# Packed attention with a gated convolution: x of two head groups in one step on eight TensorE tiles, weight parts added on GpSimd

## The chip, the cores and the metric

The kernel runs on one core of a Trainium2 chip. The metric is device time in microseconds for one execution; lower is better. The engines are called as the profile calls them: PE (TensorE's matmuls), PEld (its weight loads), DVE (VectorE), ACT (ScalarE), POOL (GpSimd) and SP (SyncE, which here only issues DMAs). SBUF is the on-chip memory, PSUM the accumulators that PE writes.

## What is computed

```python
# q, k, v: (8, 8, 576, 64)   p: (8, 8, 32, 64)   w_val, w_out: (512, 512)   conv_w: (5, 512)
def sm_attn(qq, kk, vv):
    s = scale * np.matmul(qq, kk.transpose(0, 1, 3, 2))
    a = np.exp(s - np.max(s, axis=-1, keepdims=True))
    a = a / (np.sum(a, axis=-1, keepdims=True) + 1e-09)
    return np.matmul(a, vv)
p_packed = sm_attn(p, k, v)
out = sm_attn(q, p_packed, p_packed)
x = out.transpose(0, 2, 1, 3).reshape(8, 576, 512)
gate = sigmoid(sum(conv_w[k] * xp[:, k:k + 576, :] for k in range(5)))   # xp: x with 4 zero rows in front
return gate * (x @ w_val) @ w_out
```

For each of the 8 batches and 8 heads, 32 packed queries attend to 576 keys (the first attention), the 576 queries attend to the 32 results (the second), and the joined heads x pass through a gated causal convolution between two matrix products. q, k, v and p are 32-bit floats; the three weights reach the kernel as 64-bit floats.

## The kernel before

Heads go in two groups of four (`G` = 2), since four heads of 32 packed rows fill 128 partitions. A batch passes through streams of steps, each named by a letter (and the batch's number) in a table `ORDER`: K, V, Q, P load; `k` and `q` transpose keys and queries on PE (tiles `kpt`, `qpt`) and copy them with ACT; `a` is the first attention (scores `s`, their maxima `nb` on DVE, the exponential on ACT, transposes `at`, products `pv`, the result `ppd`); `p` turns `ppd` into `ppT`; `s` and `t` are the second attention (scores `s` on PE, a transpose of 32x32 blocks to `t` and the maxima `mx` on DVE, a subtraction on POOL, the exponential on ACT, sums `sm` and reciprocals `rs` on DVE, a product on POOL, a transpose back to `a` on DVE and its split into a high part `a2h` and a low part `a2l`); `w` multiplies the packed results by `w_val` (tile `wp`, split into `wph` and `wpl`); `x` computes x itself (function `mixed`, tile `xp`); `g` is the gate (four DVE steps of multiply and add into `sig` after one on ACT, then a tanh, for each of four chunks of 128 channels); `v` is the value product (tile `val`, times `sig`, split into `gvh` and `gvl`); `o` is the output product and its store. L, W, C and O load the weights and convert the 64-bit words: three or four DVE steps per 128 rows make two parts, `top` and `words`, which PE adds into PSUM by two products with the identity (`summed`; tiles `wv_sum` and `wo_sum`).

The order of every engine's instructions is the order of this table: `InOrder` ties each instruction to the one before it on its engine, and a letter in `ORDER` runs one step of its stream (`x0.2` runs two). The engines then run freely, each in its own order, and wait for each other by semaphores. Before the bar `|` in the table the weights' staging memory is alive, behind it `gvh` and `gvl`. SP's DMAs stand in the same order, in one queue.

x is the product of `ppd` (32 packed rows by 64 channels of one head, the weights) and the attention `a` (32 by 288 columns, half the sequence at a time). One head needs a tile of 32 rows and 64 columns of the PE array, of which there are eight: four row groups by two column groups. Before, a step takes the four heads of one group, with head `hl` on row group `hl` and column group `hl % 2`. It writes one buffer of the PSUM ring `big`, which has two buffers of two banks each, and which `scores`, `wp` and `val` use too; ACT then copies it into `xp`. A batch has four such steps and four copies. The ring of `xp` has two tiles, one for each group.

A matmul of 32-bit floats appears as two records in the profile: a step of four x tiles has 8, a step of eight score tiles 16. In the rows that list the instructions in order it is one instruction.

Of the kernel before, what the change touches and what calls it, by code (L numbers as in the profile page):

```python
# [39 lines left out]
 'xp': 2}  # L40
# [6 lines left out]
x0 K0.2 P0 L0.2 Q0 L0.2 V0.2 k0 Q0 L0 k0.2 P1 k0.4 P2 W0 k0.2 W0 K1 k0.2 a0 W0 k0.2 W0 a0 k0 K1 W0.2 a0 W0 L0 a0  # L47
W0 q0 W0 a0 q0.2 W0 q0.2 Q1 a0.3 W0 q0 W0.2 a0 W0 L0 a0 W0 a0.2 W0 a0 W0.5 L0 a0 W0.2 a0.3 V1 W0 a0.6 W0.3 a0 V1
C0 L0 W0 C0 q0 C0 p0 k1 q0 p0 C0 P3 q0 k1 C0 s0 q0 C0 q0 w0 s0 q0 Q1 s0 k1 C0 s0 w0 C0 k1.2 w0 s0.2 k1.2 t0 K2
k1.4 a1 k1 s0 t0 k1 O0 a1 k1 k2 K2 O0 a1.2 P4 t0 O0 t0 x0 a1 k2 q1 O0 a1.3 O0.2 a1 s0 q1 x0 t0 s0 O0 q1 a1 O0.2  # L50
x0 a1 O0 q1 a1 s0 q1 O0 a1 t0 Q2 q1 x0.2 a1 g0 O0 t0 O0.2 a1 V2 a1 t0 O0 g0 a1 t0 x0 O0.2 g0 a1.6 O0 x0 g0 x0 a1
V2 t0 p1 v0 g0 p1 x0 O0 g0 s1 O0 g0 v0 q1 s1 w1 q1 g0 k2 O0.2 w1 s1 g0 s1 k2 w1 O0 k2 q1 O0.2 s1 g0 k2.2 q1.2 O0
K3 k2.2 g0 q1 Q2 a2 k2 O0 x1 g0 s1 t1 k2 g0 q2 k2.2 O0 q2 t1 q2 a2 K3 k2 k3 q2 s1 q2 P5 a2 O0.2 q2 g0 Q3 t1 | v0
g0 a2 t1 x1 s1 O0 k3 v0 s1 k3 x1 a2 k3.2 O0 a2.3 g0 s1 v0 a2 t1 k3 t1 q2 a2 x1 q2 v0 t1 a2 q2 g0 a2 v0 k3 x1 K4
k3 t1 g0 v0.2 q2 g0 v0 q2 a2 Q3 q2 g0 a2 v0 g0 t1 k3 V3 a2.3 k3 t1 k3 a2.2 g0 k3.2 a2.2 k3 v0 K4 v0 a2 g0.2 x1
k4 x1 g1 P6 v0 a2 g1 v0 x1.2 V3 g1 a2 p2 v0 x1 v1 p2 g1.2 o0 g1.2 v1 g1 v1 a3 v1 o0 s2 g1 o0.2 a3 s2 a3 g1 s2 a3
o0 g1 s2 v1 o0 k4 a3 g1 a3.2 x2 q3 v1 s2 a3 s2 a3 t2 q3 k4 v1 w2 k4 s2 t2 g1 k4 v1 q3 w2 v1 s2 k4 q3 w2 s2 k4 q3
k4 K5 o0 t2 q3 Q4 s2 g1 t2 g1 t2 k4 o0 q3 g1 a3 k4 o0.2 q3 t2 a3 g1 t2 g1 k4 g1 v1 a3 x2 o0 t2 a3 o0 a3 v1 g1
# [48 lines left out]
def packed_attention_gated_conv(  # L107
# [97 lines left out]

    def words_of(nm, src, rows):
        words = tile_of("words", [P, DM, 2], U32, f"{nm}_words", stage)[:rows]
        each = rows // len(src)  # L210
        for n, s in enumerate(src):
            sp.dma_start(
                words[n * each : n * each + each].rearrange("a b c -> a (b c)"), s.bitcast(U32)
            )
# [431 lines left out]
```

## Time and profile before

| | |
|---|---|
| median of 3 runs | 319.11 us (318.81 to 319.12) |
| the profiled execution: its time, its span | 318.79 us, 316.7 us |
| PE busy | 292.0 us, 92% |
| PEld busy | 210.3 us, 66% |
| DVE busy | 256.5 us, 81% |
| ACT busy | 211.1 us, 67% |
| POOL busy | 44.8 us, 14% |
| DMA | 43.50 MB, mean 137 GB/s |

The span runs from the first to the last instruction of the profiled execution; its device time holds 2.1 us more. A share of busy time is a mean over stages in which different engines are full. Nearly all instructions are recorded under line 90, the helper that ties them in order, so the rows are told apart by their tiles: `x<-a,ppd` is the product that makes x, `xp<-x` its copy.

### The profile page before, as it was taken

What the parts mean: (1) busy time and instruction counts of PE and PEld (TensorE: products, weight loads), DVE (VectorE), ACT (ScalarE), POOL (GpSimd) and SP (SyncE); (2) the same over time, 40 slices, a digit from 0 to 9 for tenths busy, and PEclk for the clock granted to TensorE, in tenths of its full rate; (3) what the DMA queues carried; (4) which work ended last, traced back from release to release, by engine and by line L of the source; (5) the groups of instructions that cost most, each with busy time, mean ns of one, the idle gap of its engine ahead of it and who ended that gap; (6) DMA issues with size and microseconds to landing.
All of it is one profiled execution on the core that took longest, in us unless ns stands there. A gap on an engine that the chain in (4) does not pass through costs nothing.

```text
span 316.7 us, 7391 instructions
## 1 busy us (share of the span) xinstructions
PE 292.0 (92%) x3028; PEld 210.3 (66%) x3028; DVE 256.5 (81%) x404; ACT 211.1 (67%) x428; POOL 44.8 (14%) x55
## 2 busy tenths in 40 slices
PE   0878987988899999999999999999999999999992
PEld 0534534556766876787777867777787687767871
DVE  0336799999888987898999888997999878868761
ACT  1564787688966778768867786688766955455431
POOL 1000131113002210033003202210032100220000
PEclk9999999999999999999999999999999999999998
DMA  8999999999991479328652866415242021111005
GB/s 180 220 231 226 243 256 218 214 229 192 192 198 74 107 188 224 83 81 216 151 139 73 208 185 120 123 55 129 58 141 68 2 66 36 66 68 47 20 2 167
DMA packets 42476, 43.50 MB, mean 137 GB/s; under 512 B 6085, under 2 KB 36805, under 8 KB 42442
## 3 DMA queue, kind: packets, MB, share of 16 engines
q1 hardware_dynamic: 42442, 43.02, 58.8%
q8 instruction: 24, 0.39, 0.6%
q14 instruction: 10, 0.08, 0.1%
HBM read 33.57 MB, written 9.44 MB: 136 GB/s over the span
## 4 chain that ended last, share of the span: by engine, by line
PE 69%; DVE 15%; ACT 6%; DMA 5%; issue 1%; SPq 0%; POOL 0%; POOLq 0%; DVEq 0%; ACTq 0%
PE o L90 26%; PE val L90 13%; DVE sig L90 6%; PE s L90 5%; PE x L90 5%; PE kpt L90 4%; PE qpt L90 4%; PE pv L90 3%; DMA qm<-in_q_dram 3%; PE at L90 3%; PE wv_sum L90 2%; PE wp L90 2%; DMA p<-in_p_dram 2%; DVE sm L90 2%; ACT sig L90 2%; DVE wo_words L90 1%
## 5 line engine op out<-in xcount | busy, mean ns | idle before, releaser
L90 DVE SCALAR_TENSOR_TENSOR sig<-xp,cw,sig 128x576 f32<-128x576 f32 x128 | 107.5, 840 | 5.9 <-ACT sig L90 4.8
L90 PE MATMUL o<-woh,gvh 128*128 128x512 f32 x144 | 59.0, 409 | 0.1
L90 PE MATMUL o<-wol,gvh 128*128 128x512 f32 x144 | 56.5, 393 | 0.0
L90 PE MATMUL o<-woh,gvl 128*128 128x512 f32 x144 | 56.5, 392 | 0.1
L90 PE MATMUL val<-a2h,wph 128*128 128x288 f32 x128 | 39.9, 312 | 0.0
L90 POOL TENSOR_TENSOR t<-t,mx 128x576 f32<-128x576 f32 x16 | 22.9, 1432 | 110.3 <-DVE mx L90 110.3
L90 PE MATMUL val<-a2h,wpl 128*128 128x288 f32 x128 | 37.9, 296 | 0.0
L90 PE MATMUL val<-a2l,wph 128*128 128x288 f32 x128 | 37.8, 295 | 0.0
L90 ACT COPY osb<-o 128x512 f32<-128x512 f32 x34 | 19.9, 584 | 25.1 <-PE o L90 17.0
L90 ACT ACTIVATE sig<-sig 128x576 f32<-128x576 f32 x32 | 22.0, 689 | 21.3 <-DVE sig L90 21.3
L90 DVE SCALAR_TENSOR_TENSOR sig<-sig,val 128x576 f32<-128x576 f32 x32 | 24.0, 751 | 12.6 <-ACT sig L90 7.8
L90 PEld LDWEIGHTS o<-woh,gvh 128*128 128x128 f32 x144 | 27.1, 188 | 8.8 <-ACT osb L90 2.4
L90 PEld LDWEIGHTS o<-woh,gvl 128*128 128x128 f32 x144 | 27.1, 188 | 6.7 <-DVE gvl L90 0.5
L90 PEld LDWEIGHTS o<-wol,gvh 128*128 128x128 f32 x144 | 27.1, 189 | 4.6
L90 PEld LDWEIGHTS kpt<-ident,km 96*128 96x128 f32 x192 | 20.2, 151 | 11.9 <-issue 4.8
L90 ACT COPY qT<-qpt 128x384 f32<-128x384 f32 x48 | 23.2, 486 | 6.8 <-PE qpt L90 6.5
L90 ACT CAST gvh<-sig 128x576 fp32r<-128x576 f32 x32 | 21.6, 676 | 9.0 <-DVE sig L90 7.9
L90 POOL TENSOR_TENSOR t<-t,rs 128x576 f32<-128x576 f32 x16 | 19.9, 1244 | 54.6 <-DVE rs L90 47.3
L90 PE MATMUL kpt<-ident,km 96*128 96x96 f32 x192 | 25.7, 266 | 2.0 <-DVE wol L90 1.0
L90 DVE TENSOR_TENSOR gvl<-sig,gvh 128x576 fp32r<-128x576 f32 x32 | 24.6, 769 | 2.5 <-ACT gvh L90 2.3
L90 PEld LDWEIGHTS val<-a2h,wph 128*128 128x128 f32 x128 | 24.2, 189 | 2.7 <-issue 0.9
L90 ACT COPY kT<-kpt 128x384 f32<-128x384 f32 x48 | 22.9, 483 | 4.2 <-PE kpt L90 4.0
(82 smaller groups left out, 504.9 us busy)
## 6 DMA issues: line engine op xcount, KB each, us to landing
km<-in_k_dram SPq DMA_DIRECT2D x16, 576.0 KB, 6.1
qm<-in_q_dram SPq DMA_DIRECT2D x16, 576.0 KB, 7.0
vm<-in_v_dram SPq DMA_DIRECT2D x16, 576.0 KB, 7.3
out_dram<-osb SPq DMA_DIRECT2D x24, 256.0 KB, 2.1
wv_words<-in_moe_w_val_dram SPq DMA_DIRECT2D x8, 256.0 KB, 9.1
wo_words<-in_moe_w_out_dram SPq DMA_DIRECT2D x4, 512.0 KB, 13.6
out_dram<-osb SPq DMA_DIRECT2D x8, 192.0 KB, 3.4
p<-in_p_dram SPq DMA_DIRECT2D x16, 64.0 KB, 7.9
```

Source lines behind the costliest of these rows:

```text
L90: made = getattr(self.engine, op)(*args, **kw)
```

## The change

There are four parts.

1. `mixed` takes both groups in one step: for each half of the sequence it asks for two `big` buffers and issues eight matmuls, the heads of group 1 on the other column group, so that all eight tiles of 32x64 are used. Two copies follow. A batch has two such steps and four copies, and both `xp` tiles are cleared ahead of them.
2. The crossed column groups put the two heads of each chunk of group 1 in exchanged order in the channels. The weights follow: the right half of `w_val`'s columns is stored crosswise, the right half of `conv_w` is loaded by two more DMAs, and each 128 rows of `w_out` by two DMAs of 64 rows instead of one.
3. `w_val`'s two parts are added by POOL (two additions of 128x256 for each 128 rows) straight into `wv`, in place of PE's sum in PSUM and ACT's copy. `w_out`'s parts are still added by PE.
4. The ring of `xp` has three tiles, that of `mx2` two, `eps` is half as wide, and the table `ORDER` is another.

```diff
- 'xp': 2}
+ 'mx2': 2,
+ 'xp': 3}
...
-x0 K0.2 P0 L0.2 Q0 L0.2 V0.2 k0 Q0 L0 k0.2 P1 k0.4 P2 W0 k0.2 W0 K1 k0.2 a0 W0 k0.2 W0 a0 k0 K1 W0.2 a0 W0 L0 a0
+x0 L0 x0 K0 L0 P0 K0 L0 W0 L0 W0.2 V0 W0 Q0 W0 P1 W0 L0 W0 V0 W0 k0 L0 W0 k0.2 W0 k0.2 Q0 W0 P2 k0.2 W0 k0.2 K1
...
+    def halves(c):
+
+        return (c * P, c * P + D) if c < NC // 2 else (c * P + D, c * P)
...
-        st["words", "cw"] = words_of("cw", [conv_w], NT)
+        st["words", "cw"] = words_of("cw", [conv_w[:, : DM // 2]], NT, DM // 2)
+        swapped = conv_w[:, DM // 2 :].bitcast(U32).rearrange("n (c t d) -> n c t d", c=2, t=2)
+        to = st["words", "cw"][:, DM // 2 :, :].rearrange("n (c t d) x -> n c t (d x)", c=2, t=2)
+        for t in range(2):
+            sp.dma_start(to[:, :, t], swapped[:, :, 1 - t])
...
-            st["words", "wo"][c] = words_of(f"wo{c}", [w_out[c * P : c * P + P, :]], P)
-            yield
...
+            st["words", "wo"][c] = words_of(f"wo{c}", [w_out[r : r + D, :] for r in halves(c)], P)
+            yield
...
-            ps = summed(f"wv{c}", words)
-            yield
-            act.copy(wv[:, c, :], ps)
+            for low in range(2):
+                cs = slice(low * DM // 2, low * DM // 2 + DM // 2)
+                to = wv[:, c, cs].rearrange("a (x t d) -> a x t d", x=2, t=2)
+                ins = [
+                    x[:, cs].rearrange("a (x t d) -> a x t d", x=2, t=2)
+                    for x in (st["top", f"wv{c}"], words[:, :, 0].bitcast(F32))
+                ]
+                pool.tensor_tensor(to[:, :, ::-1] if low else to, *ins, op=ALU.add)
...
-            for half in range(2):
-                hc = slice(half * HS, half * HS + HS)
-                pp, a2 = st["ppd", b], st["a2", b]
-                xps = big(f"x_{b}_{g}_{half}")
+        for half in range(2):
+            hc = slice(half * HS, half * HS + HS)
+            pp, a2 = st["ppd", b], st["a2", b]
+            xps = [big(f"x_{b}_{g}_{half}") for g in range(G)]
+            for g in range(G):
                 for hl in range(4):
+                    at = D * ((hl + g) % 2)
                     pe.matmul(
-                        xps[D * (hl % 2) : D * (hl % 2) + D, hl // 2, :HS],
+                        xps[g][at : at + D, hl // 2, :HS],
                         pp[heads[hl], g, 0, :],
                         a2[heads[hl], g, hc],
                         start=True,
                         stop=True,
                     )
-                yield
-                act.copy(xp[:, :, half, PAD:], xps[:, :, :HS])
+            yield
+            for g in range(G):
+                act.copy(st["xp", b, g][:, :, half, PAD:], xps[g][:, :, :HS])
                 yield
```

Three places show what the new order does. In the names below, `x_1_0` is x of group 1, half 0, and a number at a name's end counts buffers.

The first is the start of SP's queue, where the loads of batch 0 and of the weights stand. Before:

```order
L90 DMA km_0_80<-in_k_dram 96x4x384
L90 DMA km_1_82<-in_k_dram 96x4x384
L90 DMA p_84<-in_p_dram 128x2x64 x2
L90 DMA wv_words<-in_moe_w_val_dram 64x1024 x4
L90 DMA qm_0_93<-in_q_dram 96x12x128
L90 DMA wv_words<-in_moe_w_val_dram 64x1024 x4
L90 DMA vm_0_101<-in_v_dram 96x4x384
L90 DMA vm_1_103<-in_v_dram 96x4x384
L90 DMA qm_1_108<-in_q_dram 96x12x128
L90 DMA cw_words<-in_moe_conv_w_dram 5x1024
```

And in the changed kernel:

```order
L91 DMA wv_words<-in_moe_w_val_dram 64x1024 x2
L91 DMA km_0_85<-in_k_dram 96x4x384
L91 DMA wv_words<-in_moe_w_val_dram 64x1024 x2
L91 DMA p_90<-in_p_dram 128x2x64 x2
L91 DMA km_1_93<-in_k_dram 96x4x384
L91 DMA wv_words<-in_moe_w_val_dram 64x1024 x4
L91 DMA vm_0_105<-in_v_dram 96x4x384
L91 DMA qm_0_108<-in_q_dram 96x12x128
L91 DMA p_111<-in_p_dram 128x2x64 x2
L91 DMA cw_words<-in_moe_conv_w_dram 5x512
L91 DMA cw_words<-in_moe_conv_w_dram 5x2x128 x2
L91 DMA vm_1_122<-in_v_dram 96x4x384
```

The first rows of `w_val` moved ahead of K and p; K's second group and p moved behind a quarter or two of `w_val`; V's second group is now behind p of batch 1 and `conv_w`.

The second is PE's queue in batch 0, from the first of the first attention's transposes (`at`) on. Before:

```order
L90 MATMUL at_0_0_230<-ident,a_0_0_182 96x128 x2
L90 MATMUL wv_sum<-wv_top,ident 128x512
L90 MATMUL wv_sum<-wv_words,ident 128x512
L90 MATMUL at_0_1_243<-ident,a_0_0_182 96x128 x2
L90 MATMUL at_0_2_249<-ident,a_0_0_182 96x128 x2
L90 MATMUL wv_sum<-wv_top,ident 128x512
L90 MATMUL wv_sum<-wv_words,ident 128x512
L90 MATMUL pv_0_263<-vm_0_101,a1t_0_229 32x64 x24
```

And in the changed kernel:

```order
L91 MATMUL at_0_0_226<-ident,a_0_0_202 96x128 x2
L91 MATMUL at_0_1_234<-ident,a_0_0_202 96x128 x2
L91 MATMUL at_0_2_239<-ident,a_0_0_202 96x128 x2
L91 MATMUL pv_0_243<-vm_0_105,a1t_0_225 32x64 x24
L91 MATMUL at_1_0_276<-ident,a_0_1_219 96x128 x2
```

The sums of `w_val` are gone from between the transposes and products of the first attention; they are POOL's now.

The third is PE's queue at the last batch's x, where output chunks and values of the batch before surround it. Before, the step of group 0 and half 0 has an output chunk on each side:

```order
L90 MATMUL o_0_3643<-woh,gvl 128x512
L90 MATMUL x_0_0_3666<-a_7_3636,ppd_3251 64x288 x4
L90 MATMUL o_1_3676<-woh,gvh 128x512
L90 MATMUL o_1_3676<-wol,gvh 128x512
L90 MATMUL o_1_3676<-woh,gvl 128x512
```

And in the changed kernel:

```order
L91 MATMUL o_8_3615<-woh,gvl 128x512
L91 MATMUL x_0_0_3635<-a_7_3497,ppd_3113 64x288 x4
L91 MATMUL x_1_0_3636<-a_7_3497,ppd_3113 64x288 x4
L91 MATMUL x_0_1_3654<-a_7_3497,ppd_3113 64x288 x4
L91 MATMUL x_1_1_3655<-a_7_3497,ppd_3113 64x288 x4
L91 MATMUL val_3_3668<-a2h_3145,wph_3242 128x288
L91 MATMUL val_3_3668<-a2h_3145,wpl_3243 128x288
```

The four groups of x matmuls, which had output chunks and values between them, now follow each other as two joint steps, with the values of the batch before (`val_3`) moved behind them.

More of the change, by code (lines that the diff above doesn't have):

```diff
@@ L417, in weighted @@
             dve.tensor_reduce(s3, t3, axis=AX.X, op=ALU.add)
-            dve.tensor_tensor(s3, s3, eps[:, : n * NBLK], op=ALU.add)
+            dve.tensor_tensor(s3, s3, eps, op=ALU.add)
             dve.reciprocal(r3, s3)
@@ L514, in value @@
                         pe.matmul(
-                            vps[:, half, :HS], w[:, g, cols], x[:, g, hc], start=(n == 0), stop=(n == 5)
+                            vps[:, half, :HS], w[:, g, n4 * P : n4 * P + P], x[:, g, hc], start=(n == 0), stop=(n == 5)
                         )
```

82 lines of the change are left out of this document (43 added, 39 removed).

## The prediction

> **What bounds the kernel now.** I read the page first, then busy time by stage, then the chain of waits.
>
> ```profile
> PE 292.0 (92%) x3028; PEld 210.3 (66%) x3028; DVE 256.5 (81%) x404; ACT 211.1 (67%) x428; POOL 44.8 (14%) x55
> ...
> PE   0878987988899999999999999999999999999992
> ...
> DVE  0336799999888987898999888997999878868761
> ```
>
> The average (PE 92%, DVE 81%) hides two stages: PE's row reaches a steady 9 only after a quarter of the span, while DVE's row has a weak start. The next view cuts the span where that happens; a row begins with the stretch and its length. The cuts are DVE's first instruction (12.25), the first s block of the second attention reaching DVE (34.85), the first `o` matmul (91.07), DVE's last `gvl` (307.82) and the last matmul (311.10).
>
> ```profile
> core 0 of [0], span 316.7 us
> core 0: us, PE busy (x) PEld busy (x) DVE busy (x) ACT busy (x) POOL busy (x), PEclk, DMA share, GB/s
> 0.00:12.25 12.25, 3.05 (x19) 3.08 (x20) 0.00 (x0) 3.22 (x6) 0.80 (x8) 1.00 0.91 194
> 12.25:34.85 22.60, 19.17 (x207) 9.11 (x206) 13.34 (x28) 12.78 (x31) 0.00 (x0) 1.00 1.13 228
> 34.85:91.07 56.22, 50.01 (x638) 31.58 (x639) 52.92 (x91) 44.93 (x98) 10.91 (x11) 1.00 1.09 219
> 91.07:311.10 220.03, 219.81 (x2170) 166.53 (x2168) 190.26 (x287) 149.56 (x294) 33.07 (x36) 1.00 0.40 103
> 311.10:316.70 5.60, 0.00 (x0) 0.00 (x0) 0.01 (x1) 0.58 (x1) 0.00 (x0) 0.84 0.57 198
> ```
>
> From 91.07 to 311.10 PE is busy for 219.81 of 220.03 us: whatever leaves PE there leaves the span, as long as DVE (190.26, 86.5%) follows. Before that PE has holes, and DVE is the engine to watch: nothing for 12.25 us, 13.34 of the next 22.60, then 52.92 of 56.22 (94%). DMA is saturated all along (share near 1.1, some 220 GB/s). So the start is DVE work that begins late, behind loads.
>
> ```profile
> 2.21 6.86 DMA p<-in_p_dram
> ...
> 29.09 0.89 PE pv L90 x48
> 29.97 2.12 PE wv_sum L90 x4
> ...
> 33.68 1.11 PE s L90 x16
> ```
>
> The chain of waits (start, length) says why 34.85 is so late: PE's in-order queue has the `wv` sums between batch 0's scores, `pv` and second scores.
>
> **The x step.** These rows are TensorE's instructions in time order (start, length), then the time of all x matmuls ahead of and behind the first `o`.
>
> ```profile
> 146.09 0.71 PE L90 MATMUL x<-a,ppd 32*64 32x288 f32 x8
> 146.74 0.55 PE L90 MATMUL kpt<-ident,km 96*128 96x96 f32 x4
> 147.12 0.49 PE L90 MATMUL qpt<-ident,qm 96*128 96x96 f32 x4
> 147.54 0.72 PE L90 MATMUL x<-a,ppd 32*64 32x288 f32 x8
> 148.19 0.42 PE L90 MATMUL at<-ident,a 128*96 128x128 f32 x2
> 148.37 0.38 PE L90 MATMUL val<-a2h,wph 128*128 128x288 f32 x1
> ...
> 156.59 0.72 PE L90 MATMUL s<-kT,pT 64*32 64x288 f32 x16
> ```
>
> ```profile
> 0.00:91.07 91.07, 5.72 (x64) 1.68 (x64) 5.14 (x8) 1.00 1.08 218
> 91.07:311.10 220.03, 17.16 (x192) 4.95 (x192) 15.41 (x24) 1.00 0.40 103
> ```
>
> A step of four x tiles (8 records) holds PE 0.65 us, from 146.09 to the next start at 146.74, and its records take 0.71. A step of eight s tiles of the same 288 columns (16 records) takes 0.72, so it too holds PE 0.65. Time goes by columns, not by tiles, as long as tiles run side by side. The joint step has eight tiles of the x shape: nearest row, the s step, 0.65. The ends: 0.65, and 1.30 if the groups take turns. Behind the first `o` stand 24 steps (192 records) now and 12 joint ones after: 24 x 0.65 - 12 x 0.65 = **-7.8**. The 8 steps ahead of it save PE time where DVE decides: 0.
>
> By the issue order one kpt, two at and three s steps move from behind the first `o` to ahead of it. At 0.38 us (146.74 to 147.12), 0.18 (148.19 to 148.37) and 0.65 that is **-2.7** behind it.
>
> **The buffers of the joint step.** Both `big` buffers of PSUM must be free for one joint step, where before each half step took one and the other could still be in use.
>
> ```profile
> L90 DVE SCALAR_TENSOR_TENSOR sig<-sig,val 128x576 f32<-128x576 f32 x32 | 24.0, 751 | 12.6 <-ACT sig L90 7.8 <-PE val L90 4.4
> ...
> L90 ACT COPY xp<-x 128x576 f32<-128x576 f32 x32 | 20.6, 642 | 0.3
> ```
>
> A buffer comes free after an x copy (0.64), or a `sig` times `val` (0.75). In batch 7's order the two joint steps stand next to each other: the second waits for both copies, 2 x 0.64 = 1.28 less the overlap; in batch 3's a val step ends only a kpt and an at, 0.6 us, before the second joint step. Behind a waiting x on PE's queue stand kpt, at, o and val, which ACT and DVE wait for. Ends: 0, and 12 x 1.28 = 15. In most places other PE steps stand between, so I take a third of a microsecond each: **+4**.
>
> **The start.** With `w_val` first in SP's queue, DVE's first work is no longer behind K, p and their 6.86 us. Half a megabyte at the first stage's 194 GB/s is 2.7 us; with some 2 us of issue and lag and ACT's scaling of well under 1 us, DVE starts near 5.5 (an estimate). p comes some 1 to 2 us later than at 9.07, K of group 1 too. Then batch 0's second scores need the last V block: w_val 2.10, K 1.18, p 0.26, Q 0.59, V 1.18 = 5.3 MB, which the two stages' 194 and 228 GB/s deliver by 25.1. The `pv`, two copies, transposes and s behind it took 33.68 - 29.09 = 4.6 with a `wv` sum of 2.1 in them: 28.3, so DVE has the block at 28.5 instead of 34.85: **-6.3** (ends: 0 if p and K eat it, -8). From there to the first `o` DVE now does 52.92. By the order it has one gate step, two nb and a pair of small ones more to do before the first `o`:
>
> ```profile
> L90 DVE SCALAR_TENSOR_TENSOR sig<-xp,cw,sig 128x576 f32<-128x576 f32 x128 | 107.5, 840 | 5.9 <-ACT sig L90 4.8
> ...
> L90 DVE TENSOR_REDUCE nb<-s 128x1 f32<-128x576 f32 x16 | 12.0, 750 | 1.4 <-PE s L90 1.3
> ```
>
> That is 0.84 + 2 x 0.75, some 2.4 in all; but two `wo` steps, half of that, now stand ahead of the block: **+1.2**. The first `o` comes at 91.07 - 6.3 + 1.2 = 86.0.
>
> **POOL's adds.** PE loses the `wv` sums, ACT their copies:
>
> ```profile
> 0.00:91.07 91.07, 8.91 (x16) 2.39 (x16) 2.34 (x4) 1.00 1.08 218
> ```
>
> These are the `wv` sums alone: 8.91 us of PE, all in the start, where PE has holes: 0 beyond what the start's term holds. POOL gets eight adds of 128x256, and has nothing else before 34.85.
>
> ```profile
> 47.59 0.69 DVE L90 SCALAR_TENSOR_TENSOR wo_top<-wo_top,wo_words 128x512 uint32<-128x512 uint32 x1
> ...
> 49.71 1.16 POOL L90 TENSOR_TENSOR t<-t,rs 128x576 f32<-128x576 f32 x1 [2.69 <-DVE rs L90]
> 49.88 1.53 DVE L90 SCALAR_TENSOR_TENSOR wo_words<-wo_words 128x512 f32<-128x512 uint32 x1
> ```
>
> From 1.16 us for 576 columns an add is 0.52, eight are 4.1. The last two rows show a price: a DVE step of the kind that took 0.69 took 1.53 beside POOL. At worst that is 4.1 us of DVE, in a stretch where DVE idles 22.60 - 13.34 = 9.3: 0, worst end +4.1. The Trainium skill ("SBUF — State Buffer", "SBUF: two separate sides") calls the pair of ports that both engines share an exclusive lock, held for a whole instruction; those rows agree, and by that rule without idle time the sum would be 4.1 higher.
>
> **Small edits.** Two more DMAs for conv_w and four more for w_out cost issue time on SP in a queue that waits for DMA anyway: 0; uncovered, six issues of at most half a microsecond. The third `xp` buffer and its early memsets take away a wait:
>
> ```profile
> DVE a L90 <- POOL xp L90: 2.8, 3, 1.3
> ```
>
> Worth 0 to -2.8; I take 0, since DVE's late work in the last batch is covered by PE in the new order. `mx2`, `eps`: 0.
>
> **Sum.** Span 86.0 + (220.0 - 7.8 - 2.7 + 4) + 5.6 = 305.1; outside the span the profiled execution has 318.79 - 316.7 = 2.1: 307.2. The median of the runs, 319.11, lies 0.3 above this execution: **307.5**. Differences under 0.2% (0.6 us) can't be told from none.
>
> **Rivals.**
> - DVE becomes the bound. It keeps 190.26 - 2.4 = 187.9 of work behind the first `o`, in 213.5: 88%, against 86.5% now. If 86.5% is all that the back and forth with ACT and POOL allows, the stage takes 217.2: 311.2. For it: DVE's 9s. Against: 94% between 34.85 and 91.07.
> - The start isn't shorter, since DMA is saturated either way and K and p come later: 6.3 back, 313.8. Against: DVE's idle 12.25 us are plain to see.
> - Everything meets: a start of -8 and no stall: 301.8.
> - The eight tiles take turns: 12 x 0.65 back, 315.3. The Trainium skill ("TensorEngine Tiling (Array Packing)", "Gotcha 1: PSUM Pressure") says that different row tiles can't access one PSUM bank at the same time, and x has row tiles 0 and 1 in one bank. The trace speaks against it: the four x tiles already share banks so, and hold PE no longer than the s step, whose row tiles have a bank each.
> - Slower: the joint step starves PE. The wait for both buffers costs on average over 1.35 us at each of the 12 joint steps (twice the ACT copy), 0.33 + 11.6/12, because ACT and DVE, in order, reach the release late; at 1.5 it is 18 instead of 4, 321.5. Against: the x steps at 146.09 and 147.54 follow each other by 1.45 us now, with no hole on PE.
>
> **Chances.** Forecast (303 to 310.5) 0.45; DVE the bound 0.14; start no shorter 0.13; everything meets 0.12; tiles take turns 0.06; no change within 0.2% 0.04; slower 0.06. Faster: 0.90. The range from 301 to 315 leaves out the last two and part of the turn-taking.
>
> **What would show it.** Right: x in half as many steps of 0.65 to 0.75; DVE's first instruction near 5.5 and the first `o` near 86; PE over 97% busy from there to its end. Wrong: joint steps near 1.3; PE waiting for "ACT xp" or "DVE sig" at x for more than 4 us in all; the first `o` still at 91 with DVE waiting for DMA; PE holes that end with DVE at over 90%.

## The result, and the profile after

The changed kernel takes 326.32 us (median of 4 runs, 326.03 to 328.66), the one before 319.12 (318.81 to 319.44): 1.024 times as long, with an interval of 1.020 to 1.028. Forecast were 307.5 us and a gain. The profiled execution is the longest of the four (328.66; its span is 326.8, those of the others 324.2 to 324.7), so some 2.4 us of what follows belong to that one execution.

The page after, busy time first, then the rows of 40 slices, with the granted clock of TensorE in the last:

```profile
PE 287.5 (88%) x3012; PEld 212.6 (65%) x3012; DVE 257.9 (79%) x404; ACT 209.9 (64%) x424; POOL 50.9 (16%) x63
...
PE   0377959798868999999999999999999899999993
...
DVE  0456697889969987989797898986999799888821
...
PEclk9999698999997999999999999999999999999998
```

PE needs 4.5 us less than before and the span is 10 longer. The steady 9 comes two slices later, and the clock has three weak slices where it had none. Cut at the same events as before (DVE's first instruction, the first block `t`, the first `o`, the last matmul; the stretch up to 7.63 is left out):

```profile
7.63:35.41 27.78, 17.17 (x210) 12.11 (x218) 15.35 (x30) 12.10 (x29) 5.69 (x8) 0.93 1.12 209
35.41:103.31 67.90, 56.49 (x699) 35.47 (x684) 57.66 (x96) 49.92 (x109) 11.28 (x12) 0.93 0.98 199
103.31:321.31 218.00, 213.80 (x2114) 165.07 (x2112) 184.88 (x279) 145.36 (x283) 33.09 (x35) 1.00 0.39 100
321.31:326.80 5.49, 0.00 (x0) 0.00 (x0) 0.04 (x1) 0.58 (x1) 0.00 (x0) 0.84 0.58 201
```

DVE does start earlier, 7.63 for 12.25, but hands nothing on: its first block is at 35.41 (34.85 before). The third stretch has grown from 56.22 to 67.90 us, and DVE is busy for 57.66 of it, 85% where it was 94%. The first `o` comes at 103.31, 12.2 us later than before and 17.3 later than forecast. From there to the last matmul it is 218.0, 2.0 less than before. PE gave up 6.0 us there (219.81 to 213.80) and got 4.0 of them back as holes (0.2 to 4.2).

The x matmuls alone, ahead of the first `o` and behind it:

```profile
0.00:103.31 103.31, 4.34 (x64) 1.29 (x64) 5.04 (x8) 0.93 1.00 200
103.31:321.31 218.00, 11.97 (x192) 3.87 (x192) 14.90 (x24) 1.00 0.39 100
```

Behind the first `o` x holds PE for 11.97 us where it held it for 17.16. PE's rows show the joint step at its best and at its worst:

```profile
189.85 0.74 PE L91 MATMUL x<-a,ppd 32*64 32x288 f32 x16
190.52 0.55 PE L91 MATMUL kpt<-ident,km 96*128 96x96 f32 x4
...
284.90 0.74 PE L91 MATMUL x<-a,ppd 32*64 32x288 f32 x16
286.38 1.26 PE L91 MATMUL x<-a,ppd 32*64 32x288 f32 x16 [0.73 <-ACT xp L91]
287.85 0.40 PE L91 MATMUL val<-a2h,wph 128*128 128x288 f32 x1 [0.22 <-ACT xp L91]
```

Eight tiles run side by side: 0.67 us to the next start, as four did in 0.65. But the second joint step of the last batch waits 0.73 for the copies of the first, and its 1.26 holds another wait inside, since the first group's matmuls go when one buffer is free and the second group's when the other is. Of the twelve steps behind the first `o`, six are undisturbed (those at 154.75, 189.85, 196.16, 219.84, 255.55 and 284.90). Twelve at 0.74 would be 8.9, so 3.1 us of waiting lie inside the records of the others; the holes ahead of x, and of the value product behind it, are 2.5 more.

Where the start goes is seen in five places. First, batch 0's first attention, whose p and K now stand behind parts of `w_val`. The last scores of it before, then p's transpose (the first thing PE does), the same scores and the first products after:

```profile
16.82 0.72 PE L90 MATMUL s<-kT,pT 64*32 64x288 f32 x16
```

```profile
12.60 0.66 PE L91 MATMUL pTt<-ident,p 128*128 128x128 f32 x2 [12.60 <-DMA p<-in_p_dram]
...
20.33 1.21 PE L91 MATMUL s<-kT,pT 64*32 64x288 f32 x16 [0.86 <-ACT kT L91]
...
24.14 1.51 PE L91 MATMUL pv<-vm,a1t 96*32 96x64 f32 x48 [1.15 <-ACT a1t L91]
```

p's transpose waits for its DMA until 12.60, where it started at 9.20 before, and the last keys wait for K until 15.99. So the scores come 3.5 us later. They also take 1.21 us for 0.72, and `pv` 1.51 where the next one, at 29.57, takes 0.88. With no sums of `w_val` in between, the first `pv` is still 2.9 us earlier than before (27.08); the second is 0.6 later than before (29.01). Neither waits for V.

Second, PE's rows ahead of the first block:

```profile
29.57 0.88 PE L91 MATMUL pv<-vm,a1t 96*32 96x64 f32 x48 [0.72 <-ACT pT L91]
32.08 0.55 PE L91 MATMUL cwps<-ident,cw_top 5*128 5x5 f32 x4 [1.64 <-DVE cw_top L91]
32.56 0.69 PE L91 MATMUL ppTt<-ident,ppd 128*128 128x128 f32 x2
33.73 1.22 PE L91 MATMUL s<-qT,ppT 64*32 64x288 f32 x16 [0.47 <-ACT ppT L91]
```

`conv_w`'s transposes (`cwps`) now stand ahead of `ppTt` on PE's queue and wait for DVE's conversion, and the scores behind them take 1.22 us, not 0.72. The third place explains that; the number behind POOL's is the granted clock:

```profile
28.00:30.00 2.00, 1.28 (x40) 1.08 (x42) 1.04 (x2) 1.81 (x5) 0.43 (x1) 1.00 1.00 189
30.00:32.00 2.00, 0.45 (x32) 0.28 (x21) 1.83 (x4) 0.37 (x1) 0.00 (x0) 0.86 1.21 202
32.00:34.00 2.00, 1.45 (x14) 1.01 (x22) 0.18 (x1) 0.71 (x2) 0.00 (x0) 0.50 1.23 218
34.00:36.00 2.00, 2.00 (x32) 0.45 (x16) 1.63 (x3) 0.23 (x1) 0.00 (x0) 0.50 1.15 246
36.00:38.00 2.00, 2.00 (x17) 1.42 (x10) 1.96 (x5) 1.25 (x2) 0.77 (x1) 0.50 1.01 147
```

PE, half idle, is granted half its clock, and that lasts until 38, though PE is busy all the time from 34 on. Before, two of the `wv` sums stood in these holes (29.90 to 32.07 us); PE was busy for 3.9 of the 4 us from 28 to 32, at a clock of 1.00.

Fourth, the gate. Its first DVE step and the x steps that feed it, before (two rows) and after (five rows):

```profile
42.35 0.71 PE L90 MATMUL x<-a,ppd 32*64 32x288 f32 x8 [0.56 <-DVE a L90]
...
52.27 0.78 DVE L90 SCALAR_TENSOR_TENSOR sig<-xp,cw,sig 128x576 f32<-128x576 f32 x1
```

```profile
52.66 0.74 PE L91 MATMUL x<-a,ppd 32*64 32x288 f32 x16
...
55.48 1.13 PE L91 MATMUL wo_sum<-wo_top,ident 128*128 128x512 f32 x2
56.45 1.17 PE L91 MATMUL wo_sum<-wo_words,ident 128*128 128x512 f32 x2
57.54 0.74 PE L91 MATMUL x<-a,ppd 32*64 32x288 f32 x16
...
61.21 0.81 DVE L91 SCALAR_TENSOR_TENSOR sig<-xp,cw,sig 128x576 f32<-128x576 f32 x1
```

A joint step needs the attention of both groups, so batch 0's first x is 10 us later than group 0's alone was. The second joint step follows 4.9 us behind the first, since a sum of `w_out`'s parts stands ahead of it on PE's queue. The gate starts at 61.21, 8.9 us later.

Fifth, the rest of the way to the first `o`:

```profile
88.06 0.71 PE L91 MATMUL x<-a,ppd 32*64 32x288 f32 x8
90.14 0.71 PE L91 MATMUL x<-a,ppd 32*64 32x288 f32 x8 [1.37 <-ACT xp L91]
...
92.08 0.72 PE L91 MATMUL x<-a,ppd 32*64 32x288 f32 x8
93.55 0.71 PE L91 MATMUL x<-a,ppd 32*64 32x288 f32 x8 [0.76 <-ACT xp L91]
94.92 1.21 PE L91 MATMUL s<-kT,pT 64*32 64x288 f32 x32 [0.66 <-DVE sig L91]
...
97.69 0.42 PE L91 MATMUL at<-ident,a 128*96 128x128 f32 x2 [0.87 <-ACT pT L91]
99.09 0.42 PE L91 MATMUL at<-ident,a 128*96 128x128 f32 x2 [0.97 <-ACT ppT L91]
...
100.39 0.61 PE L91 MATMUL val<-a2h,wph 128*128 128x288 f32 x1
```

Batch 1's x falls apart into four group steps that pass one after another through one buffer, since the other is held by a value block of batch 0 whose `sig` times `val` stands behind them in time (DVE, 94.11). Then the scores of batches 2 and 3 that the new order has moved ahead of the first `o` run as a chain from 94.92 to 100.39, with nothing beside them, and PE's clock falls once more (0.44 for a value product that takes 0.30).

### The profile page after: what moved, and what is told of

It is laid out like the page before. It is cut to its first block, busy times and chain, and to the rows that moved or that the text cites. A ratio compares the mean times of both kernels' runs of the same rounds, so it can differ in the third digit from the quotient of the medians.

```text
span 326.8 us, 7382 instructions
## 1 busy us (share of the span) xinstructions
PE 287.5 (88%) x3012; PEld 212.6 (65%) x3012; DVE 257.9 (79%) x404; ACT 209.9 (64%) x424; POOL 50.9 (16%) x63
## 4 chain that ended last, share of the span: by engine, by line
PE 58%; DVE 22%; ACT 11%; DMA 3%; issue 3%; SPq 1%; POOL 0%; DVEq 0%; ACTq 0%
PE o L91 24%; PE val L91 12%; DVE sig L91 10%; PE s L91 4%; PE qpt L91 3%; DMA km<-in_k_dram 3%; PE x L91 3%; PE pv L91 3%; ACT sig L91 3%; PE kpt L91 2%; PE wo_sum L91 2%; PE at L91 2%; DVE sm L91 2%; ACT xp L91 2%; PE wp L91 1%
## 5 line engine op out<-in xcount | busy, mean ns | idle before, releaser
L91 DVE SCALAR_TENSOR_TENSOR sig<-xp,cw,sig 128x576 f32<-128x576 f32 x128 | 108.6, 848 | 9.0 <-ACT sig L91 7.8
L91 PE MATMUL qpt<-ident,qm 96*128 96x96 f32 x192 | 25.5, 261 | 0.6 <-ACT qT L91 0.6
```

The lines of the kernel that those rows point to most:

```text
L91: made = getattr(self.engine, op)(*args, **kw)
```

## The experiments

Times are medians, each beside the kernel before on the same chip; the ratio is worked out from the single times and not from the two medians. "Stage two" is the stretch from the first `o` to the end of the last matmul of the profiled execution, "gate" the first DVE step of batch 0's gate.

| kernel | median us | before | ratio (95%) | block t_0 | gate | first o | stage two |
|---|---|---|---|---|---|---|---|
| before | 319.12 | | | 34.85 | 52.27 | 91.07 | 220.0 |
| after | 326.32 | 319.12 | 1.024 (1.020, 1.028) | 35.41 | 61.21 | 103.31 | 218.0 |
| e1_halves | 318.87 | 319.00 | 0.999 (0.996, 1.001) | 35.38 | 52.74 | 91.55 | 220.0 |
| e2_pool | 317.99 | 319.00 | 0.998 (0.995, 1.002) | 31.75 | 49.78 | 88.92 | 220.0 |
| e3_hybrid | 329.08 | 319.00 | 1.030 (1.026, 1.034) | 31.85 | 60.49 | 102.45 | 218.0 |
| e4_turns | 327.89 | 319.00 | 1.028 (1.024, 1.033) | 33.51 | 59.69 | 101.80 | 219.4 |
| e5_adapted | 350.31 | 319.73 | 1.098 (1.093, 1.103) | 31.91 | 58.70 | 105.18 | 239.7 |
| e6_x_later | 326.70 | 319.73 | 1.026 (1.019, 1.032) | 33.70 | 58.80 | 101.21 | 218.0 |
| e7_warm | 326.40 | 319.73 | 1.021 (1.015, 1.027) | 33.02 | 56.87 | 98.96 | 218.1 |
| e8_cheap_x | 317.61 | 319.73 | 0.994 (0.992, 0.997) | 34.09 | 51.46 | 90.70 | 218.5 |
| e9_late | 323.59 | 319.94 | 1.013 (1.010, 1.016) | 32.43 | 50.41 | 96.92 | 218.0 |
| e10_late_warm | 324.61 | 319.94 | 1.016 (1.013, 1.019) | 32.50 | 51.47 | 99.29 | 218.0 |
| e11_pool_warm | 319.05 | 319.94 | 0.998 (0.995, 1.002) | 34.02 | 52.40 | 93.95 | 219.9 |
| e12_start_mended | 332.98 | 319.94 | 1.043 (1.038, 1.048) | 33.97 | 56.38 | 112.88 | 218.0 |
| e13_scores_later | 332.70 | 320.00 | 1.040 (1.036, 1.044) | 34.23 | 60.00 | 96.76 | 229.8 |
| e14_late_scores_later | 327.43 | 320.00 | 1.023 (1.020, 1.027) | 31.60 | 51.57 | 91.29 | 227.9 |
| e15_scores_later_warm | 331.39 | 320.00 | 1.037 (1.034, 1.041) | 34.05 | 57.71 | 94.47 | 229.9 |
| e16_all_mended | 334.67 | 320.00 | 1.047 (1.043, 1.051) | 32.88 | 56.53 | 95.78 | 229.6 |
| e17_last_four | 320.98 | 318.77 | 1.006 (1.004, 1.009) | 31.92 | 52.09 | 92.14 | 222.0 |
| e18_last_four_turns | 322.15 | 318.77 | 1.010 (1.007, 1.013) | 31.49 | 49.80 | 91.11 | 222.9 |

Every kernel that keeps the changed order and the eight tiles side by side behind the first `o` has a stage two of 218.0 to 218.1, however its start went.

### The small parts alone: the DMAs, and GpSimd's sums

Kernel before, with the six more DMAs of part 2:

```diff
-words_of(f"wo{c}", [w_out[c * P : c * P + P, :]], P)
+words_of(f"wo{c}", [w_out[r : r + D, :] for r in (c * P, c * P + D)], P)
```

> The kernel before, with each 128 rows of w_out loaded by two DMAs of 64 rows and conv_w by three DMAs; nothing else changed. Theory 'smaller DMAs': in the changed kernel the DMA moved some 210 GB/s in its first 55 us against 225 before, because the w_out loads were cut; then this kernel is 3 to 5 us slower (322 to 324). Rival 'only the order': the rate fell for another reason, and this kernel stays at 319 within 1 us.

Measured: 0.999, the first `o` 0.5 us later. The small DMAs cost nothing that can be told.

Kernel before, with GpSimd's sums in place of PE's for `w_val`:

```diff
-ps = summed(f"wv{c}", words)
-act.copy(wv[:, c, :], ps)
+pool.tensor_tensor(wv[:, c, cs], *ins, op=ALU.add)
```

> The kernel before, with w_val's parts added by POOL (eight adds) in place of PE's sums and ACT's copies; order as before. Theory 'PE goes cold': without the 8.9 us of sums in the start PE has long holes, its granted clock falls to one half there as in the changed kernel (0.50 from 31 to 38 us), and the kernel is no faster or slower, 319 to 322. Rival 'the sums were in the way': PE's queue is freed, batch 0's second scores come 3 to 5 us earlier and the kernel takes 314 to 317.

Measured: no difference that can be told (0.998), though block t_0 is 3.1 us and the first `o` 2.2 us earlier in the profiled execution, one of the shortest of ten. Nine of the ten lie between 316.6 and 320.6, those of before between 317.9 and 320.8. Each expectation had a part: the block came earlier, and without the `wv` sums PE has holes and its clock stands at 0.50 from about 23 to 33 us. An addition of 128x256 takes GpSimd 0.73 us (5.7 for eight in the changed kernel), not the forecast 0.52, in time that it has.

### The changed start

Changed kernel, its table up to batch 0's first x step replaced by the old one:

```diff
-x0 L0 x0 K0 L0 P0 K0 L0 W0 L0 W0.2 V0 W0 Q0 W0 P1 W0 L0 W0 V0 W0 k0 ...
+x0 K0.2 P0 L0.2 Q0 L0.2 V0.2 k0 Q0 L0 k0.2 P1 k0.4 P2 W0 k0.2 W0 K1 ...
```

> The changed kernel's code, with the issue order of the kernel before up to the first x step of batch 0, then the rest in the changed order. Theory 'the start': the loss lies in the changed order of the start (first o at 103.3 us where 86 was forecast); with the old start the first o comes at 91 to 95 and the kernel takes 314 to 319. Rival 'the joint step': both buffers at once, POOL's adds and PE's lower clock cost the time wherever the start's order comes from; first o at 100 or later, 323 to 328.

Measured: 329.08. The old order brings block t_0 to 31.85, but the joint x of batch 0 still comes at 51.38 and the gate at 60.49. The time is that of the rival and a little more: an early block is worth nothing as long as x waits for both groups and `w_out`'s sums stand between the joint steps.

Changed kernel, with fourteen small products with the identity to fill PE's holes ahead of `cwps` (6), batch 1's second scores (4) and batch 2's `pTt` (4):

```diff
+warm(6)
 cps = one("cwps")
```

> The changed kernel with 14 small products (128 columns) of the identity with itself on PE, into the output buffer that nothing uses yet, at the three places where PE idles longest between 30 and 48 us. Theory 'PE goes cold': the granted clock stays at 1.00 where it was 0.50 from 31 to 38 and from 49 to 52 us, the first o comes 3 to 5 us earlier, 321 to 324. Rival 'DVE and DMA set the start': clock up, but the first o at 102 to 104 and 325 to 328.

The granted clock was 1.00 from 30 to 50 us in the profiled execution. Its first `o` is 4.3 us earlier, but it is the shortest of four (324.19; the others 325.3 to 327.6), and the median, 326.40, is that of the changed kernel. So the clock of these 20 us isn't the loss; whether it held in the other three executions isn't shown.

Changed kernel, batch 1's x behind the value block that holds its buffer:

```diff
-... x1 a2 P6 g0 t1 a2 x1 g0 x1 q2 t1 x1 V3 a2 q2 Q3 g0 x1 g0 a3 g1 v0 x1 x2 a3 v0 g1 ...
+... a2 P6 g0 t1 a2 g0 q2 t1 V3 a2 q2 Q3 g0 g0 v0 x1.6 a3 g1 ...
```

> The changed kernel with one place of its table altered: batch 1's two joint x steps and their copies stand behind batch 0's last value step (the sig times val that frees a big buffer) and not ahead of it. Theory 'a held buffer': in the changed kernel val_3 holds one of the two buffers there, the four groups of x pass one by one through the other (PE idles 3.4 us between 90 and 100, DVE 3.2), so that x runs here as 16 records twice and the first o comes 3 to 6 us earlier than 103.3; 320 to 323. Rival 'it is late anyway': the wait moves to batch 1's gate, 325 to 327.

Measured: 326.70. x comes in three pieces instead of four, with one wait of 3.0 us for the copies in front of it, and the clock falls there (0.50 from 92 to 96): one wait for another, as the rival had it.

All of these at once, and `w_out`'s last two quarters behind the first gates:

```diff
-... O0 g0 O0 q1 g0 a1 O0 g0.2 O0 g0 ...
+... g0 q1 g0 a1 g0.2 O0.2 g0 O0 a1 O0 q1 O0 ...
```

> The changed kernel with three things in its start mended at once: the small products that keep PE's clock up (as in e7_warm), x of batch 1 behind value block 3 of batch 0 (as in e6_x_later), and the conversions of w_out's last two quarters moved behind the first gates of batch 0. Theory 'order of the start': the clock gives 4.3 us of the first o's 103.31 (e7_warm 98.96), x of batch 1 about 2 (e6_x_later 101.21), the conversions 3 to 4 (the gate of batch 0 starts at 53 to 56, in the changed kernel at 61.21): first o at 93 to 95, time 316 to 319. Rival 'the late loads of p and K pace it': the gate still starts behind 57, first o at 97 or later, time 322 or more.

Measured: 332.98, slower than any mend alone. The gate starts at 56.38, only 0.5 earlier than with the small products alone, and the conversions, packed together, wait for each other in a ring of DVE, PE and ACT: between 60 and 80 DVE is busy for 10.2 us only. (The profiled execution took 337.97, so its times are read roughly.)

Changed kernel and its joint step, but the old order up to the first `o` and x of batches 0 and 1 group by group:

```diff
 for g in range(G):
     ...
+    if b < 2:
+        yield from steps(b, [[g]])
+if b >= 2:
+    yield from steps(b, [range(G)])
```

> The changed kernel, but up to the first output product the order of the kernel before (sums of w_val on GpSimd, x of batches 0 and 1 taken group by group); from there on the changed kernel's order with its joint x steps for batches 2 to 7. Theory 'the start is the miss': first o near 89 (88.92 in e2_pool), then the changed kernel's 217.9 us to the last matmul and 5.6 behind it: span 312.4, time 314.5, 1.4% under the kernel before. Rival 'the joint steps need what the changed start had done ahead': the eleven scores' and values' steps that the changed kernel has done more by its first o are missing, PE gets holes behind the junction, stage two is 220 or more, and the time is 317 to 319, no better than e2_pool's 318.

Measured: 323.59, against 326.32 for the changed kernel (1.013 and 1.024 to before), and over both expectations. The gate is back at 50.41 and the last value product ahead of the first `o` ends at 91.3, where the kernel before begins its first `o`. Then come the steps that the changed order has moved ahead:

```profile
91.27 0.71 PE L89 MATMUL s<-kT,pT 64*32 64x288 f32 x16
93.77 0.72 PE L89 MATMUL s<-kT,pT 64*32 64x288 f32 x16 [1.79 <-ACT a L89]
94.42 0.55 PE L89 MATMUL kpt<-ident,km 96*128 96x96 f32 x4
94.81 0.65 PE L89 MATMUL at<-ident,a 128*96 128x128 f32 x4
96.27 0.72 PE L89 MATMUL s<-qT,ppT 64*32 64x288 f32 x16 [0.82 <-ACT a L89]
96.92 0.50 PE L89 MATMUL o<-woh,gvh 128*128 128x512 f32 x1
```

They take 5.65 us, of which PE waits 2.6 within the rows shown; stage two is 2.0 shorter for them and for the joint steps together.

With products that fill the hole ahead of batch 0's first values, on this kernel and on e2_pool:

```diff
 pv = one(f"pv_{b}_{g}")
+if b == g == 0:
+    warm(14)
```

> e9_late with fourteen 128-column products of the identity in front of batch 0's first values (where PE waits for V, 19.3 to 23.1 in e2_pool, and its granted clock then stands at 0.50 until 33). Theory 'the clock costs the start': the granted clock stays at 1.00 through the first 40 us, first o comes 2 to 4 us earlier than in e9_late, and the time is 311 to 313. Rival 'V and the conversions pace the start anyway': the clock stays up, but first o moves by less than 0.7 us and the time is that of e9_late.

> The kernel before with GpSimd's sums for w_val (e2_pool) and the same fourteen products in front of batch 0's first values. Theory 'the clock costs the start': first o at 85 to 87 (88.92 in e2_pool), stage two unchanged at 219.6, time 314 to 316. Rival 'V and the conversions pace it': first o at 88.3 to 89, time 317 to 318 as in e2_pool.

Measured: 324.61 for e9_late's 323.59, 319.05 for e2_pool's 317.99, and the runs of each pair overlap. In neither did the clock hold through the first 40 us (0.83 from 20 to 40). Both expectations of a gain were wrong, and what a clock that holds would be worth there isn't shown.

### Steps moved ahead of the first output

The moved steps put behind the first `o`, between two chunks, in the changed kernel and in e9_late; then with e7's products, and with e6's edit too:

```diff
-... a3 v0 g1 a3.3 k4 p2 g1 a3 k4 a3.2 p2 g1 a3.2 k4 s2 v0 a3 v1 g1 s2 g1.2 o0 s2 ...
+... v0 g1 p2 g1 p2 g1 v0 v1 g1.3 o0 a3.3 o0.2 a3.2 k4 o0 a3 k4 a3.2 o0.2 a3.2 k4 s2 a3 s2.2 ...
```

> The changed kernel with one part of its order undone: the first eleven steps of batch 3's first attention, three of its K and the first two of batch 2's second scores stand behind the first output product and between the next two chunks, as in the kernel before, not ahead of it. Theory 'moved ahead is exposed': between 94.92 and 103.31 PE waited 2.5 us in that stretch and its clock fell to 0.50 for the last twelve value products (1.4 us more); behind output chunks the waits are covered: first o at 97 to 98.5, the time 3 to 5 us less, 321.5 to 323.5. Rival 'it is given back': the same waits come between the output chunks or in batch 1's values, first o is earlier by 5 but stage two longer by as much, time 325.5 to 327.

> e9_late with the same edit. Theory 'moved ahead is exposed': first o at 91.2 (where e9_late stood before those steps), time 2.5 to 4 us under e9_late's 323.6, so 319.5 to 321, about the kernel before and e2_pool plus nothing: the joint steps in stage two are worth no more than 1.5 us. Rival 'given back': 323 to 324.

> e13_scores_later with the small products that keep PE's clock up (e7_warm). If the terms add up: the first o's 103.31 less 4.3 (clock; 1.4 of it the same as in e13) and less 5: 95 to 96, time 319.5 to 322. If the clock costs nothing that another wait doesn't take: that of e13.

> e15 with x of batch 1 behind value block 3 of batch 0 as well (e6_x_later). If the terms add up: first o 93 to 94.5, time 318 to 320.5. If x of batch 1 then only waits for that value block in its turn (as e6_x_later's unchanged time says): the time of e15.

All four were slower than the kernels that they mend, and "given back" had the sign right, though not the size. In the first two the first `o` came 6.5 and 5.6 us earlier, as expected, but stage two grew by 11.8 and 9.9. In the last two nothing added up: with the small products the time is 331.39 (332.70 without), with e6's edit too 334.67. First the two largest waits in e13_scores_later, then its stage two and that of e14_late_scores_later:

```profile
102.14 0.72 PE L89 MATMUL s<-kT,pT 64*32 64x288 f32 x16 [1.78 <-ACT a L89]
...
113.54 1.50 PE L89 MATMUL pv<-vm,a1t 96*32 96x64 f32 x48 [3.06 <-ACT a1t L89]
```

```profile
96.76:326.58 229.82, 220.29 (x2170) 168.84 (x2168) 190.24 (x289) 149.91 (x293) 34.30 (x35) 0.99 0.38 97
```

```profile
91.29:319.17 227.88, 218.49 (x2170) 167.68 (x2168) 189.63 (x287) 150.41 (x293) 34.01 (x35) 0.99 0.38 98
```

Each has 9.4 to 9.5 us of holes there, the changed kernel 4.2; the two waits shown are most of the difference. PE is also busy for 6.5 us more in e13_scores_later: 2.7 is what the steps were forecast to hold it, and from 97 to 117 its granted clock is 0.83. The products of two output chunks don't cover the chain when three and more of its steps stand in a row between them.

### The joint step by itself

Changed kernel, the tiles of both groups on the same column groups, so that they take turns:

```diff
-at = D * ((hl + g) % 2)
+at = D * (hl % 2)
```

> The changed kernel with head hl on column group hl % 2 for both groups of heads, so that a joint step uses four tiles twice instead of eight once (the exchanged channels and the weights that follow them are undone); same order, same buffers. Theory 'eight tiles pay in the PE-bound stage': 12 steps behind the first o at 0.65 us more each, 7.8 us more, 333 to 335. Rival 'PE waits there anyway': x steps wait for buffers and copies, and the four-tile form costs 0 to 3 us, 326 to 329.

Measured: 327.89, in the rival's range. A step takes 1.20 us (the one at 50.88) and not 0.74, so x of stage two holds PE for 14.91 us (11.97); stage two grows by 1.4 of these 2.9.

Kernel before, x of group 1 not computed, two cheap full products in its place, some 0.3 us a step instead of 0.65:

```diff
+for bank in range(2 * g):
+    pe.matmul(xps[:, bank, :HS], woh[:, 0, :P], st["ah", b][:, 0, hc], start=True, stop=True)
-for hl in range(4):
+for hl in range(4 - 4 * g):
```

> The kernel before, in which x of group 1 is not computed: two full products of 288 columns in one pass take the place of its four tile products, so that such a step holds PE some 0.3 us in place of 0.65; order, copies and buffers as before. It prices PE time in the PE-bound stage: 12 such steps behind the first o. Theory 'PE-bound': the whole saving reaches the span, 4 us, 314 to 316. Rival 'PE is busy but not alone': less than half does, 317 to 319.

Measured: 0.994, the rival's time. Stage two is 218.5, 1.5 less than before, and PE is busy there for 216.6 us, 3.2 less. About half of what PE is spared arrives in the time, in the old order and without any wait for two buffers.

Old order with the joint step put where both its buffers are free, so delayed past whatever holds one:

```diff
-... v1 g1 x2.2 v1 V4 a3 k4 v1 a3 t2 g1 x2 t2 k4 g1 a3 q3 k4 K5 a3 g1 a3 q3.2 a3.2 g1 x2.2 Q4 a3 v1 g2 a3 x2 g2 x2 ...
+... v1 g1 x2.3 v1 V4 a3 k4 v1 a3 t2 g1 t2 k4 g1 a3 q3 k4 K5 a3 g1 a3 q3.2 a3.2 g1 Q4 a3 v1 x2.2 a3 x2 g2 ...
```

> The changed kernel's code (joint x step, POOL's adds, three xp tiles) with the order table of the kernel before, changed as little as the joint step needs: a joint step is issued only once the values, scores and packed values that hold a big buffer are read, and gate steps come behind their x. Theory 'the order' (the joint step pays, the changed table loses it): first o at 88 to 92, x as 16 records of 0.72 in nearly all steps, 310 to 315. Rival 'the joint step itself': both groups' attention and both buffers at once cost as much as the tiles save, 318 to 324.

Measured: 350.31, far over both expectations. The first `o` is 14.1 us later than before and stage two 19.7 longer. PE has 16.7 us of holes behind the first `o`, 3.5 of them ahead of x and 4.1 ahead of values that wait for x's copies. What must wait for both buffers holds up the values, the scores and the outputs behind it.

Last, the joint step without the other parts. Both orders have issued the same steps but one memset at the end of batch 3's x, so that is where the next kernel passes from the old order (x group by group) to the changed one (joint, batches 4 to 7); its partner has the tiles take turns:

```diff
-if b < 2:
+if b < 4:
```

> The order of the kernel before, with GpSimd's sums, up to the end of batch 3's x (x group by group), and from there the changed kernel's order with joint x steps for batches 4 to 7: the place was chosen because both orders have issued the same steps there but for one memset. Theory 'the joint step gives back most of itself': in the changed kernel 12 joint steps took 5.2 us less of PE and 2.5 us of holes in front of them came back, 0.22 each; eight of them give 1.8: 316.2 where e2_pool had 318.0. Rival 'a joint step is worth its whole 0.65 and the losses were all in the bunches': 318.0 - 5.2 = 312.8. Rival 'the order behind is the loss': 318 or more.

> e17_last_four with every head hl of both groups on column group hl % 2, so that the two groups take turns (a joint step took 1.20 in e4_turns and 0.74 in the changed kernel). If PE sets the pace where the joint steps stand: 8 x 0.46 = 3.7 us slower than e17_last_four. If half of it is hidden, as in e4_turns (1.4 of 2.9): 1.8 slower. If the joint step's worth is given back whole: no difference.

Stage two of e2_pool, e17_last_four and e18_last_four_turns, in this order (PE's time in the second column):

```profile
88.92:308.88 219.96, 219.77 (x2170) 166.42 (x2168) 190.16 (x287) 149.54 (x293) 33.07 (x36) 1.00 0.39 102
```

```profile
92.14:314.10 221.96, 218.39 (x2170) 166.04 (x2168) 190.26 (x287) 149.38 (x293) 33.74 (x36) 1.00 0.39 100
```

```profile
91.11:314.03 222.92, 220.69 (x2170) 167.46 (x2168) 189.97 (x287) 149.37 (x293) 33.77 (x36) 1.00 0.39 100
```

The same 2170 matmuls take 2.0 us longer with eight joint steps, and the changed order around them, than with none. PE's work is 1.4 less, its holes are 3.4 more, 2.3 of them ahead of x. Against before the kernel is 0.6% slower (1.004 to 1.009), e2_pool isn't; of the three expectations only 'the order behind is the loss' has this time. x alone isn't what loses: its matmuls take 13.54 us where e2_pool's take 17.14, more than the 2.3 of holes. The order of batches 4 to 7 differs from the old one in the other steps too, and no run has it without the joint steps, so the two aren't separated. The eight tiles themselves spare PE 2.3 us of stage two, not 3.7; 1.0 of them arrives there, and the medians are 1.2 apart (322.15 and 320.98, with intervals that overlap).

## Why the prediction was wrong

Against the profiled execution: the first `o` was forecast at 86.0 and came at 103.31 (+17.3), stage two at 213.5 and took 218.0 (+4.5); the rest is 5.5 for 5.6, and the median lies 2.3 below this execution where 0.3 above was added. The step that failed is **the start**, in three places.

- DVE's earlier start was to bring the first block to 28.5. DVE did start early (7.63, forecast 5.5), but the block came at 35.41. The sum let V's last block decide, and in the trace nothing waits for V. Three things were missed. p came 3.4 us later (12.60 for 9.20) where 1 to 2 were allowed for, the last keys waited for K until 15.99, and with them the first attention was late. `conv_w`'s transposes had moved ahead on PE's queue, where they wait for DVE's conversion (the row at 32.08). And PE ran as slowly as at half its clock (1.21 us for scores that took 0.72). Even e2_pool, with the old order of loads, reached 31.75 only.
- From the block to the first `o` the sum took DVE's 52.92 plus 1.2 and the 94% of before. It was 57.66 at 85% in 67.9 us. x of the first two batches was costed at 0, "where DVE decides". But a joint step can't start before both groups' attention, so the gate comes 25.8 us after the block and not 17.4. e3_hybrid, with an early block and a joint x, has 28.6; e9_late, with x by groups, 18.0. Two things differ between those two, x and what stands between it and the gate: in the changed kernel a sum of `w_out` lies between the two joint steps. The part of each isn't separated.
- One kpt, two at and three s moved ahead were booked as -2.7 behind the first `o`. They are a chain of scores, exponentials and transposes that took 5.65 us with nothing beside it on PE (e9_late). Behind the first `o` in a bunch they cost more still (e13, e14), while the order before hides them with 0.2 us of holes in its whole stage two. So it isn't ahead or behind alone that decides. That single steps of the chain, laced between output and value products, would be hidden fits the kernel before; how fine the lacing must be was not tried.

**Stage two** was right in its mechanism and off in a size. The joint step takes 0.74 as forecast, and the twelve would have saved 17.16 - 8.9 = 8.3 (forecast 7.8). The wait for both buffers cost 3.1 + 2.5 = 5.6 (forecast 4). That leaves -2.7 for -3.8; of the 2.7 for moved steps nothing is left, and some 0.7 more is lost in holes and records that I can't assign. In e17_last_four, where no steps had moved ahead of the first `o`, x gains too, and stage two is 2.0 longer all the same; that loss is not at x, and what in the order of batches 4 to 7 costs it stays open.

**Small terms.** The DMAs at 0 were right (e1). GpSimd's sums "beyond the start: 0" were right for the time (e2), but taking the `wv` sums from "where PE has holes" wasn't free of effect: with them batch 0's scores at 16.82 and `pv` at 27.08 took 0.72 and 0.88 us, without them 1.21 and 1.51 in the changed kernel and e9_late. An addition was forecast at 0.52 and takes 0.73.

**Rivals.** "Slower: the joint step starves PE" had the sign, but not the place: its waits came to 5.6 / 12 = 0.47 us a step, far under the 1.35 from which it was to decide (the sum that stands there, 0.33 + 11.6/12, gives 1.30). "The start no shorter" named the stage, and put its first `o` at 86.0 + 6.3 = 92.3, 11 us too early. The tiles don't take turns: eight of them, two row groups to a bank, take 0.74, so the bank rule that stood for it in the prediction doesn't show here. Where they are made to, a step takes 1.20. "DVE the bound" is out: it is busy for 184.88 of 218.0 us, 85%.

What the runs leave open: how much of the 8.4 us between block and gate is the joint x and how much the order of `w_out`'s conversion. e7_warm, with the small products, has 23.9 between the two, e12_start_mended, which also moves the last two quarters of the conversion, 22.4; both keep the joint x, and e12's is an execution 5 us above its median. Neither comes near the 17.4 of before.

## What to carry to other kernels

Joining two steps into one saves the engine's time but joins their conditions too: the step now waits for the later of two inputs and the later of two buffers, so price each joined step by what has to be ready, first of all in the stage where the pipeline is still filling. Work that an order moves ahead of the steady stage is no gain by itself: a chain that was hidden between long products costs its whole length, waits included, where it stands in a bunch. Before an engine is relieved, look at whether its busy time reaches the span at all (here about half did), and at whether the removed work kept it busy enough for its clock.

## What the runs showed of the hardware

TensorE's clock falls before it has been idle for long. In the changed kernel no hole from 28 to 34 us is over 1.7 us, and PE is busy for 3.2 of those 6 us, yet the granted clock was 0.50 from 32 to 38; at 98 us holes of 0.87 and 0.97 were enough:

```profile
96.00:98.00 2.00, 1.13 (x16) 0.76 (x8) 2.00 (x4) 1.18 (x4) 0.00 (x0) 1.00 1.18 206
98.00:100.00 2.00, 1.03 (x20) 0.35 (x18) 1.97 (x5) 1.93 (x6) 0.00 (x0) 0.93 0.86 158
100.00:102.00 2.00, 2.00 (x15) 1.62 (x8) 1.97 (x4) 0.97 (x2) 0.00 (x0) 0.50 0.00 0
```

The Trainium skill ("TensorE: Matmul & The Clock Gate", "Part 1: The HAM clock gate") has the clock halve after an idle window of about 3.4 us and come back after as long a busy one. The second half fits: PE is busy from 33.7 on and the clock is back between 38.0 and 38.5, some 4.5 us later. The first doesn't: half of a window's activity was too little here, with no hole as long as that (PE was busy for 1.7 of the 3.4 us ahead of the fall at 31.4, and for 1.6 ahead of the one at 99.7). Which share of a window is enough no run here shows.

The granted clock alone is also not enough at the start of these profiles. In the changed kernel it reads 1.00 from 12 to 28, and in e9_late up to 48, yet scores take 1.21 us there (at 20.33 and 30.63) and `pv` 1.51 (at 24.14 and 23.23), what they take in e2_pool where the clock reads 0.50 (at 30.35 and 23.12). Later they take 0.72 and 0.88. So like instructions have to be compared too.
